# A fused attention and GEGLU kernel: merged output stores, three tiles of x turned by DMA, halved first units, a last tile in 384 and 128 columns

## The chip, the cores and the metric

The kernel runs on one core of one Trainium2 chip. The metric is the device time of one execution in microseconds (us), as a median of several. The span of a profile is a little shorter than the time of its run (325.7 us against 327.67 us for the kernel before), because it counts from the first to the last instruction.

## The reference

Eight batches of eight heads, 576 tokens and head size 64 go through linear attention with cosine weights. The result x, 4608 tokens x 512 columns, goes through a gated feed-forward layer:

```python
q_p, k_p = phi(q), phi(k)            # relu(x)*cos, relu(x)*sin, side by side: 64 -> 128 features
kv  = einsum('bhsf,bhsd->bhfd', k_p, v);  z = sum(k_p, axis=2)
x   = (q_p @ kv) / (q_p @ z + 1e-6)  # to 4608 x 512
out = (gelu(x @ w_gate) * (x @ w_val)) @ w_out     # 512 -> 1536 -> 512, float32 out
```

## The kernel before

The feed-forward work is cut into 9 blocks of 512 tokens (n), each of 12 gate/value units (jt). While block n is worked on, the attention of batch n+1 is done between its units: `kv_unit` and `nm_unit` make tiles of x, and x must be transposed into xT before the next block can read it. q is transposed too (`turn_q`). From batch 2 on the transposes of q, and from batch 3 on all of x, are done by DMA, issued by SyncE. All loads from batch 3 on are issued by SyncE as well, and so are the output stores. SyncE issues all of these in the order of the program, on one queue.

A token s of a batch is laid out as s = 9p + j, with p from 0 to 63 and j from 0 to 8. A tile of 128 output rows holds two values of j, 64 rows each. Rows of one j lie nine rows apart in memory. The kernel stores a tile in two transfers, one for each j:

```python
def flush():
    for i, o_sb in stores:                       # one output tile of 128 rows x 512 columns
        for half in range(2):
            b, j = divmod(2 * i + half, R)       # R = 9
            dst = out[b * S:(b + 1) * S, :].rearrange("(p j) c -> j p c", j=R)[j]   # 64 x 512
            nc.sync.dma_start(out=dst, in_=o_sb[64 * half:64 * half + 64])
    stores.clear()

def turn_q(b):                                   # q of a batch, transposed by DMA
    for i in range(2):
        nc.sync.dma_start_transpose(out=qt_tile(b)[:, i]..., in_=phi["q", b][64 * i:64 * i + 64]...)

def turn_x(b, t):                                # one tile of x, transposed by DMA
    x = xs.pop((b, t))
    for blk, c, o, m in pieces(b, t):
        nc.sync.dma_start_transpose(out=xT_block(blk)[:, :, c:c + m], in_=x[o:o + m, :])

# turn_x_pe(b, t, bank, copy): the same by four TensorE transposes and a copy
# ... in the loop over blocks, n == 1:
#     turn_x_pe(b, i, 5, act_copy)     for the three first tiles of batch 2
```

Of the kernel before, what the change touches and what calls it, by code (L numbers as in the profile page):

```python
# [16 lines left out]
def kernel(  # L17
# [13 lines left out]
    nc = tc.nc  # L31

    B, H, S, D = q.shape
    F = 2 * D
    C = H * D
# [4 lines left out]
    R = S // 64  # L40
    NB = B * S // 512
# [22 lines left out]
    def bank(i):  # L64
        return ps[:, i]

    def bank16(i):
        return ps[:, i].bitcast(BF16)
# [8 lines left out]
    def load(eng, name, b, m0, m1, j0=0, j1=R):  # L77
        if (name, b) not in staged:
            staged[name, b] = inp.tile([128, NP, R * D], FP32, name=name + "f")
        eng.dma_start(  # L80
            out=staged[name, b][:, m0:m1, j0 * D:j1 * D],
            in_=rows(srcs[name], b)[:, m0:m1, j0 * D:j1 * D],
        )
# [3 lines left out]
    wo_sb = weights.tile([128, JT, C], BF16)  # L87
# [53 lines left out]
    act_copy, dve_copy, pool_copy = nc.scalar.copy, nc.vector.tensor_copy, nc.gpsimd.tensor_copy  # L141
# [35 lines left out]
    def cast_v(b, m0, m1, copy, j0=0, j1=R):  # L177
        copy(  # L178
            vx_tiles[b % 2][:, m0:m1, j0:j1, 0:D],
            staged["v", b][:, m0:m1, j0 * D:j1 * D].rearrange("p m (j d) -> p m j d", d=D),  # L180
        )
# [149 lines left out]
    def xT_block(blk):  # L331
        if blk not in xT:
            xT[blk] = xtp.tile([128, CT, BLK], BF16, name="xT")
        return xT[blk]

    def pieces(b, t):

        o = max(128 * (t + 1) - S, 0)
        c0, n = b * S + t * 128, 128 - o
        while n > 0:  # L340
            m = min(n, BLK - c0 % BLK)
            yield c0 // BLK, c0 % BLK, o, m
            c0, o, n = c0 + m, o + m, n - m

    def turn_x(b, t):
        x = xs.pop((b, t))
        for blk, c, o, m in pieces(b, t):
            nc.sync.dma_start_transpose(
                out=xT_block(blk)[:, :, c:c + m], in_=x[o:o + m, :]
            )  # L350

    def turn_x_pe(b, t, to, copy):
        x = xs.pop((b, t))
        p = bank16(to)[:, 0:CT * 128].rearrange("p (c n) -> p c n", c=CT)
        for ct in range(CT):
            nc.tensor.transpose(  # L356
                out=p[:, ct, :], in_=x[:, ct * 128:(ct + 1) * 128], identity=ident
            )
        for blk, c, o, m in pieces(b, t):
            copy(xT_block(blk)[:, :, c:c + m], p[:, :, o:o + m])  # L360
# [5 lines left out]
    def gv_unit(n, jt, c0=0, w=BLK):  # L366
        xt = xT[n]
        js = slice(jt * 128, (jt + 1) * 128)
        b0 = 2 * (turn[0] % 2)
        turn[0] += 1  # L370
        if n not in hT:
            hT[n] = ffn.tile([128, JT, BLK], BF16, name="hT")
        for g, wt in ((0, wg_sb), (1, wv_sb)):
            for ct in range(CT):
                nc.tensor.matmul(  # L375
                    bank(b0 + g)[:, 0:w],
                    lhsT=wt[:, ct, js],
                    rhs=xt[:, ct, c0:c0 + w],
                    start=(ct == 0),
                    stop=(ct == CT - 1),  # L380
                )
        gel = ffn.tile([128, BLK], FP32, name="gel")
        nc.scalar.activation(gel[:, 0:w], bank(b0)[:, 0:w], AF.Gelu)  # L383
        nc.vector.tensor_mul(  # L384
            hT[n][:, jt, c0:c0 + w], gel[:, 0:w], bank(b0 + 1)[:, 0:w]
        )

    stores = []

    def flush():  # L390
        for i, o_sb in stores:
            for half in range(2):
                b, j = divmod(2 * i + half, R)
                dst = out[b * S:(b + 1) * S, :].rearrange("(p j) c -> j p c", j=R)[j]
                nc.sync.dma_start(out=dst, in_=o_sb[64 * half:64 * half + 64])
        stores.clear()

    def o_part(i, jts, to, copy):
# [164 lines left out]
    def loads(b, names=("q", "k", "v")):  # L563
        for name in names:
            for m in (0, 2):
                load(nc.sync, name, b, m, m + 2)
# [12 lines left out]
    turn[0] = 1  # L579
    for n in range(1, NB):  # L580
        b = n + 1
        t_kv, t_nm, t_q, t_k = {1: (5, 8, 12, 12), 2: (4, 7, 7, 9), 3: (1, 5, 6, 9)}.get(
            n, (1, 2, 4, 8)
        )
        for jt in range(JT):
            if n > 2 or jt > 1:
                gv_unit(n, jt)
            else:
                for i in range(2):
                    gv_unit(n, i, jt * HALF, HALF)  # L590
                    if n == 1:
                        j = JA + 2 * jt + i
                        prep("q", b, 1, (j,), eng=nc.scalar)
                        prep("q", b, 0, (j,))
                        if jt == i == 0:
                            turn_x_pe(1, 3, 5, act_copy)
            if jt % 3 == 1:
                flush()
            if b < B:
                if n == 1 and jt == 2:  # L600
                    prep("q", b, 0, (R - 1,))
                    prep("q", b, 1, (R - 1,), eng=nc.scalar)
                    turn_q(b)
                    nm_unit(1, NT - 1)
                if n == 1 and jt == 3:
                    turn_x(1, NT - 1)
                    loads(b + 1, ("k", "v"))

                late = -(-(BLK - 64 * b) // 128)
                nms = [(b, jt - t_nm)] if 0 <= jt - t_nm < (late if n == 1 else NT) else []  # L610
                if n == 2 and jt < 2:
                    nms.append((n, 3 + jt))
                i = jt - t_nm - 1
                if 0 <= i < late:
                    if n == 1:
                        turn_x_pe(b, i, 5, act_copy)
                    else:
                        turn_x(b, i)
                for bt in nms:
                    nm_unit(*bt)  # L620
                if jt == t_kv:
                    kv_unit(b)
                i = jt - (2, 1)[n - 1] if n <= 2 else -1
                if 0 <= i < 3:
                    prep_third("k", b, i)
                if n == 2 and jt in (2, 3):
                    cast_v(b, 2 * jt - 4, 2 * jt - 2, dve_copy)
                i = jt - (10 if n == 2 else 9)
                if n > 1 and 0 <= i < 2 and b + 1 < B:
                    cast_v(b + 1, 2 * i, 2 * i + 2, dve_copy)  # L630
                if (n, jt) in q3:
                    cosines, sines_ = q3[n, jt]
                    prep("q", 3, 1, sines_, eng=nc.scalar)
                    prep("q", 3, 0, cosines)
                if n > 1 and b + 1 < B:
                    if 0 <= jt - t_q < 3:
                        prep_third("q", b + 1, jt - t_q)
                    if 0 <= jt - t_k < 3:
                        prep_third("k", b + 1, jt - t_k)
                for c, t in nms:  # L640
                    if t == NT - 1:
                        if c + 1 < B:
                            turn_q(c + 1)
                        if c + 2 < B:
                            loads(c + 2)
                        for i in range(-(-(BLK - 64 * c) // 128), NT):
                            turn_x(c, i)
            if n > 1:
                o_part(
                    4 * (n - 1) + jt // 3,  # L650
                    range(4 * (jt % 3), 4 * (jt % 3) + 4),
                    4,
                    act_copy,
                )
# [3 lines left out]


    o_sb = outp.tile([128, C], FP32, name="o_sb")  # L660
    for half, to, copy in ((0, 4, dve_copy), (1, 5, dve_copy)):
        cols = slice(256 * half, 256 * half + 256)
        for jt in range(JT):
            nc.tensor.matmul(  # L664
                bank(to)[:, 0:256],
                lhsT=hT[NB - 1][:, jt, 384:512],
                rhs=wo_sb[:, jt, cols],
                start=(jt == 0),
                stop=(jt == JT - 1),
            )  # L670
        copy(o_sb[:, cols], bank(to)[:, 0:256])  # L671
        for i, eng in ((0, nc.sync), (1, nc.scalar)):
            b, j = divmod(8 * NB - 2 + i, R)
            dst = out[b * S:(b + 1) * S, cols].rearrange("(p j) c -> j p c", j=R)[j]
            eng.dma_start(out=dst, in_=o_sb[64 * i:64 * i + 64, cols])


# [28 lines left out]
```

## Time and profile before

| | before |
|---|---|
| time, median of 6 runs | 327.67 us (327.36 to 329.83) |
| TensorE busy | 318.1 us of 325.7 (98%) |
| share of TensorE in the chain that ended last | 94% |
| end of the last matmul, end of the span | 321.9 us, 325.7 us |

These are lines of the profile page of the kernel before: the busy time of the engines, the granted TensorE clock (the share of its full speed that the chip let TensorE run at) and the DMA engines' busy share in 40 equal slices (each digit is in tenths), two of the DMA queues (packets, MB, share of 16 engines' time), the chain that ended last by engine, and the store's issues (count, KB each, median us from issue to landing).

```profile
PE 318.1 (98%) x2434; PEld 163.9 (50%) x2434; DVE 167.6 (51%) x404; ACT 161.3 (50%) x342; POOL 28.4 (9%) x43
PEclk9999999999999999999999999999999999999999
DMA  7999999988199989959978992764521111111124
...
q1 hardware_dynamic: 57632, 40.84, 54.3%
...
q10 hardware_dynamic: 160, 0.13, 0.2%
...
PE 94%; DMA 3%; DVE 1%; SPq 1%; issue 0%; DVEq 0%
...
out_dram<-o_sb SPq DMA_DIRECT2D x70, 128.0 KB, 2.5
```

TensorE is the limit. It hardly ever waits, and its mean granted clock is 0.999. The DMA row is the second thing to see: up to the 26th slice the DMA engines are nearly full in many slices, then they are almost idle. So DMA is hidden in the first two thirds, without much room. q1 is SyncE's queue and q10 ScalarE's. q10 holds two stores here, of the last tile, and their 160 packets are worth a count: 128 rows of data, and 32 packets of 4 bytes, which I read as the marks of completion: the last of them starts at 324.27 us, after the last row at 324.23 us. That is 16 marks for each store. The 3104 packets of 4 bytes on q1 add up the same way: 16 for each of 72 stores and 36 loads, 32 for each of 43 transposes.

### The profile page before, as it was taken

How to read it: one execution, taken by the hardware profiler on the slowest of the kernel's cores; microseconds unless marked ns; L12 is line 12 of the kernel's file. 1: busy time of each engine (PE TensorE's matmuls, PEld its weight loads, DVE VectorE, ACT ScalarE, POOL GpSimd, SP SyncE). 2: the span in 40 equal slices, each digit the busy share in tenths (PEclk: the TensorE clock that was granted, in tenths of full speed). 3: DMA queues.
4: the chain of work that ended last, by engine and by line, in shares of the span. 5: the costliest groups of instructions: out<-in, count | busy, mean ns of one | idle time of the engine just before them, and what ended most of it. 6: DMA issues, size and time to landing. Idle time of an engine off the chain costs nothing.

```text
span 325.7 us, 6315 instructions
## 1 busy us (share of the span) xinstructions
PE 318.1 (98%) x2434; PEld 163.9 (50%) x2434; DVE 167.6 (51%) x404; ACT 161.3 (50%) x342; POOL 28.4 (9%) x43
## 2 busy tenths in 40 slices
PE   8799999999999999999999999999999999999995
PEld 3585556556554454545544545445544444444443
DVE  5864667848845942794485448544532222222211
ACT  8764758948645833574466336642222233222220
POOL 2855462000000000000000000000000000000000
PEclk9999999999999999999999999999999999999999
DMA  7999999988199989959978992764521111111124
GB/s 275 250 191 274 307 346 340 213 128 290 30 135 369 213 102 290 306 103 179 360 160 118 309 296 47 100 108 100 90 65 40 35 32 32 34 33 32 34 64 98
DMA packets 67471, 53.17 MB, mean 163 GB/s; under 512 B 43761, under 2 KB 52721, under 8 KB 67441
## 3 DMA queue, kind: packets, MB, share of 16 engines
q1 hardware_dynamic: 57632, 40.84, 54.3%
q0 software_dynamic: 9648, 11.80, 15.8%
q8 instruction: 19, 0.31, 0.4%
q10 hardware_dynamic: 160, 0.13, 0.2%
q14 instruction: 12, 0.09, 0.1%
HBM read 37.75 MB, written 9.44 MB: 145 GB/s over the span
## 4 chain that ended last, share of the span: by engine, by line
PE 94%; DMA 3%; DVE 1%; SPq 1%; issue 0%; DVEq 0%
PE ps L375 57%; PE ps L401 28%; PE ps L281 3%; DMA qf<-in_q_dram 3%; PE ps L240 3%; PE ps L356 1%; PE ps L664 1%; SPq L80 1%; PE ps L203 1%; DVE qp L161 0%; DVE x_sb L321 0%; DVE o_sb L671 0%; DVE rec L317 0%; PE ps L139 0%; DVE den L316 0%
## 5 line engine op out<-in xcount | busy, mean ns | idle before, releaser
L384 DVE TENSOR_TENSOR hT<-gel,ps 128x512 bf16<-128x512 f32 (+2 forms) x118 | 75.5, 642 | 133.3 <-PE ps L375 129.4
L383 ACT ACTIVATE gel<-ps 128x512 f32<-128x512 f32 (+2 forms) x118 | 66.2, 562 | 107.6 <-PE ps L375 106.1
L375 PE MATMUL ps<-xT,wg_sb 128*128 128x512 bf16 (+2 forms) x472 | 112.6, 361 | 0.4 <-issue 0.4
L375 PE MATMUL ps<-xT,wv_sb 128*128 128x512 bf16 (+2 forms) x472 | 112.6, 361 | 0.0
L401 PE MATMUL ps<-wo_sb,hT 128*128 128x512 bf16 x420 | 105.9, 379 | 0.0
L375 PEld LDWEIGHTS <-wv_sb 128*128 128x128 bf16 x472 | 45.7, 98 | 47.9
L375 PEld LDWEIGHTS <-wg_sb 128*128 128x128 bf16 x472 | 44.9, 98 | 46.5 <-DMA out_dram<-o_sb 0.9
L401 PEld LDWEIGHTS <-hT 128*128 128x128 bf16 x420 | 38.4, 98 | 40.2
L410 ACT COPY o_sb<-ps 128x512 f32<-128x512 f32 x34 | 19.9, 586 | 31.3 <-PE ps L401 31.3
L159 ACT ACTIVATE qp<-qf,sin_t 128x256 bf16<-128x256 f32 x71 | 31.9, 503 | 1.0 <-DMA qf<-in_q_dram 0.8
L159 ACT ACTIVATE kp<-kf,sin_t 128x256 bf16<-128x256 f32 (+1 forms) x75 | 30.4, 477 | 0.4 <-DMA kf<-in_k_dram 0.4
L294 DVE TENSOR_TENSOR x_sb<-ps,rec 128x512 bf16<-128x512 f32 x38 | 26.3, 691 | 1.3
L161 DVE TENSOR_SCALAR qp<-qf,cos_t 128x256 bf16<-128x256 f32 x71 | 21.8, 355 | 4.2 <-ACT kv_sb L249 3.3
L161 DVE TENSOR_SCALAR kp<-kf,cos_t 128x256 bf16<-128x256 f32 x63 | 18.1, 347 | 0.0
L281 PEld LDWEIGHTS <-qT 128*128 128x128 bf16 x304 | 14.5, 98 | 7.1
L281 PE MATMUL ps<-kv_sb,qT 128*128 128x65 bf16 x304 | 16.0, 194 | 0.0
L249 ACT CAST kv_sb<-ps 128x260 bf16<-128x260 f32 x14 | 4.6, 382 | 13.1 <-PE ps L240 13.1
L139 PE MATMUL ps<-dummy 128*128 128x512 bf16 x30 | 8.9, 434 | 1.5 <-POOL dummy L113 1.5
L240 PEld LDWEIGHTS <-kp 64*128 64x128 bf16 x504 | 8.6, 94 | 3.1 <-issue 3.0
L178 DVE CAST vx<-vf 128x1152 bf16<-128x1152 f32 x12 | 9.2, 768 | 0.8 <-DMA vf<-in_v_dram 0.8
L240 PE MATMUL ps<-vx,kp 64*128 64x65 bf16 x504 | 9.5, 191 | 0.0
L293 DVE RECIPROCAL rec<-den 128x8 f32<-128x8 f32 x38 | 7.7, 203 | 1.3
(52 smaller groups left out, 95.4 us busy)
## 6 DMA issues: line engine op xcount, KB each, us to landing
out_dram<-o_sb SPq DMA_DIRECT2D x70, 128.0 KB, 2.5
kf<-in_k_dram SPq DMA_DIRECT2D x12, 576.0 KB, 6.8
vf<-in_v_dram SPq DMA_DIRECT2D x12, 576.0 KB, 8.9
qf<-in_q_dram SPq DMA_DIRECT2D x10, 576.0 KB, 5.0
qf<-in_q_dram POOLq DMA_DIRECT2D x4, 576.0 KB, 12.1
kf<-in_k_dram POOLq DMA_DIRECT2D x4, 576.0 KB, 12.8
vf<-in_v_dram POOLq DMA_DIRECT2D x4, 576.0 KB, 10.8
wg_sb<-in_moe_w_gate_dram POOLq DMA_DIRECT2D x6, 256.0 KB, 8.7
```

What stands on the lines that cost most here:

```text
L139: nc.tensor.matmul(bank(to), lhsT=dummy[:, 0:128], rhs=dummy, start=True, stop=True)
L159: nc.scalar.activation(o, i, AF.Relu, scale=tab[:, j:j + 1])
L161: (eng or nc.vector).tensor_scalar(o, i, 0.0, tab[:, j:j + 1], op0=ALU.max, op1=ALU.mult)
L178: copy(vx_tiles[b % 2][:, m0:m1, j0:j1, 0:D], staged["v", b][:, m0:m1, j0 * D:j1 * D].rearrange("p m (j d) -> p m j d", d=D),)
L240: nc.tensor.matmul(bank(6 + i)[:, m * (D + 1):(m + 1) * (D + 1)], lhsT=kp[rr, m, j, :], rhs=vx[rr, m, j, :], start=(j == 0), stop=(j == R ...
L281: nc.tensor.matmul(bank(b0 + h // 4)[:, (h % 4) * (D + 1):(h % 4 + 1) * (D + 1)], lhsT=q_cols(b, t, h), rhs=kv_sb[b][:, h // 2, h % 2, :], ...
L294: nc.vector.tensor_tensor(x, nm[:, :, :, 0:D], rec[:, :, :, None].to_broadcast([128, 2, 4, D]), op=ALU.mult,)
L375: nc.tensor.matmul(bank(b0 + g)[:, 0:w], lhsT=wt[:, ct, js], rhs=xt[:, ct, c0:c0 + w], start=(ct == 0), stop=(ct == CT - 1),)
L383: nc.scalar.activation(gel[:, 0:w], bank(b0)[:, 0:w], AF.Gelu)
L384: nc.vector.tensor_mul(hT[n][:, jt, c0:c0 + w], gel[:, 0:w], bank(b0 + 1)[:, 0:w])
L401: nc.tensor.matmul(bank(to), lhsT=hT[n][:, jt, tt * 128:(tt + 1) * 128], rhs=wo_sb[:, jt, :], start=(jt == 0), stop=(jt == JT - 1),)
L410: copy(o_sb, bank(to))
```

## The change

Four things were meant to take small pieces of work from the path. Batch 2's three tiles of x go by DMA instead of TensorE, with v(3)'s load moved behind them in the queue. Block 3's first two units are done in halves of 256 columns, so that the first can begin before all of xT is there (some casts and one `kv_unit` move with it). A tile goes out in one store of 256 KB in place of two of 128 KB. The last tile is done in 384 and 128 columns, so that the final copy and store are smaller. The core of the diff:

```diff
+    def store(eng, i, o_sb, c0=0, c1=C):
+        b, j = divmod(2 * i, R)
+        if j + 1 < R:
+            dst = out[b * S:(b + 1) * S, c0:c1].rearrange("(p j) c -> j p c", j=R)[j:j + 2]
+            eng.dma_start(out=dst, in_=o_sb[:, c0:c1])          # 2 x 64 x 512  <-  128 x 512
+        else:                                                   # tiles 4, 13, 22, 31: two batches
+            for n in range(2):
+                ...                                             # 64 x 512, as before
     def flush():
         for i, o_sb in stores:
-            for half in range(2): ...
+            store(nc.sync, i, o_sb)
...
-        t_kv, ... = {..., 3: (1, 5, 6, 9)}
+        t_kv, ... = {..., 3: (2, 5, 6, 9)}
-            if n > 2 or jt > 1:
+            if n > 3 or jt > 1:
                 gv_unit(n, jt)
...
-                    loads(b + 1, ("k", "v"))
+                    loads(b + 1, ("k",))
...
-                    if n == 1:
-                        turn_x_pe(b, i, 5, act_copy)
-                    else:
-                        turn_x(b, i)
+                    turn_x(b, i)
+                    if n == 1 and i == late - 1:
+                        loads(b + 1, ("v",))
... (casts of v moved)
-    for half, to, copy in ((0, 4, dve_copy), (1, 5, dve_copy)):      # last tile: 256 + 256
+    for c0, c1, to in ((0, C - 128, 4), (C - 128, C, 5)):            # 384 + 128
...
+        store(nc.scalar if c0 == 0 else nc.sync, 4 * NB - 1, o_sb, c0, c1)
```

More of the change, by code (lines that the diff above doesn't have):

```diff
@@ L388 @@
     stores = []
+    def store(eng, i, o_sb, c0=0, c1=C):
[5 more added lines that the diff above has]
+            for n in range(2):
+                b, j = divmod(2 * i + n, R)
+                dst = out[b * S:(b + 1) * S, c0:c1].rearrange("(p j) c -> j p c", j=R)[j]
+                eng.dma_start(out=dst, in_=o_sb[64 * n:64 * n + 64, c0:c1])
     def flush():
         for i, o_sb in stores:
-            for half in range(2):
-                b, j = divmod(2 * i + half, R)
-                dst = out[b * S:(b + 1) * S, :].rearrange("(p j) c -> j p c", j=R)[j]
-                nc.sync.dma_start(out=dst, in_=o_sb[64 * half:64 * half + 64])
+            store(nc.sync, i, o_sb)
         stores.clear()
@@ L581 @@
         b = n + 1
-        t_kv, t_nm, t_q, t_k = {1: (5, 8, 12, 12), 2: (4, 7, 7, 9), 3: (1, 5, 6, 9)}.get(
+        t_kv, t_nm, t_q, t_k = {1: (5, 8, 12, 12), 2: (4, 7, 7, 9), 3: (2, 5, 6, 9)}.get(
             n, (1, 2, 4, 8)
@@ L625 @@
                     prep_third("k", b, i)
-                if n == 2 and jt in (2, 3):
-                    cast_v(b, 2 * jt - 4, 2 * jt - 2, dve_copy)
-                i = jt - (10 if n == 2 else 9)
-                if n > 1 and 0 <= i < 2 and b + 1 < B:
+                i = jt - (2 if n == 2 else 0)
+                if n in (2, 3) and 0 <= i < 2:
+                    cast_v(b, 2 * i, 2 * i + 2, dve_copy)
+                i = jt - 9
+                if n > 2 and 0 <= i < 2 and b + 1 < B:
                     cast_v(b + 1, 2 * i, 2 * i + 2, dve_copy)
@@ L660 @@
     o_sb = outp.tile([128, C], FP32, name="o_sb")
-    for half, to, copy in ((0, 4, dve_copy), (1, 5, dve_copy)):
-        cols = slice(256 * half, 256 * half + 256)
+    for c0, c1, to in ((0, C - 128, 4), (C - 128, C, 5)):
         for jt in range(JT):
             nc.tensor.matmul(
-                bank(to)[:, 0:256],
+                bank(to)[:, 0:c1 - c0],
                 lhsT=hT[NB - 1][:, jt, 384:512],
-                rhs=wo_sb[:, jt, cols],
+                rhs=wo_sb[:, jt, c0:c1],
                 start=(jt == 0),
@@ L670 @@
             )
-        copy(o_sb[:, cols], bank(to)[:, 0:256])
-        for i, eng in ((0, nc.sync), (1, nc.scalar)):
-            b, j = divmod(8 * NB - 2 + i, R)
-            dst = out[b * S:(b + 1) * S, cols].rearrange("(p j) c -> j p c", j=R)[j]
-            eng.dma_start(out=dst, in_=o_sb[64 * i:64 * i + 64, cols])
+        nc.vector.tensor_copy(o_sb[:, c0:c1], bank(to)[:, 0:c1 - c0])
+        store(nc.scalar if c0 == 0 else nc.sync, 4 * NB - 1, o_sb, c0, c1)
 _INS = ['q', 'k', 'v', 'moe_w_gate', 'moe_w_val', 'moe_w_out']
```

## The prediction

> **What bounds it now.** TensorE. The busy table gives it 318.1 of 325.7 us, the granted clock is 0.999, and the chain of waits is 94% TensorE (57% gate/value matmuls, 28% output matmuls). From the second output block on the chain runs without a gap: 1.73 us for a gate/value unit, 0.86 us for four output matmuls, about 33.7 us per block with attention work, 31.1 us without. DMA is hidden, but with little room: by the stretches view its busy share is 0.82 to 0.98 between 52 and 181 us.
>
> **Small items, all cheap.** Three tiles of batch 2 no longer go through TensorE: 12 transposes (16 took 0.89 us in the chain, so about 0.7 us) and three ScalarE copies of about 0.59 us, off the path. Their DMA transposes land in 3.1 us median, with some 4 us to spare. v(3) is loaded about 20 us later; its cast in the second unit of block 2 might wait 1 or 2 us. Halving two units of block 3 costs nothing (16 half matmuls took 1.75 us against 1.73 for 8 whole). The last tile in 384 + 128 columns shortens its final copy (0.42 us now) by about 0.1 us. One store instead of two saves SyncE issues of 0.59 us that nothing waits for. Alone: -1 us, within 2%.
>
> **What I think decides it: the shape of the new store.** In the built program its destination has the sizes 2 x 64 x 512, its source 128 x 512. [...] No transfer of the trace before has such a shape, so the trace neither confirms nor denies it. Of 36 tiles, 32 get this store (tiles 4, 13, 22 and 31 keep two stores).
>
> Estimate: a 2 KB store packet takes 81 to 84 ns in the trace [...], so 64 on one engine take 5.2 us. Per block with attention the two engines also carry their sixteenth of the loads (9 to 11 us by packet durations), of the q transposes (about 9 us) and of the x transposes (about 4 us): with four stores 43 us against 33.7. [...] x, q and k for later blocks wait behind stores; slack of about 10 us is used up early, then TensorE waits for transposed x or q in blocks 1 to 5. Summed and with slack deducted: about 24 us. In the last 15 us tiles 32 to 34 finish every 2.6 us but each store needs 5.2 us on the same two engines: the end slips about 11 us past the last matmul's normal end.
>
> **Predicted: 362 us, 335 to 390.** Faster by over 2%: 0.03, within 2%: 0.10, slower: 0.87.
>
> **What would show it.** Stores landing in 6 us or more instead of 2.5; the DMA share at the end near 2/16 = 0.12 and some 10 us of it after the last matmul; TensorE gaps of several us in blocks 1 to 5, with transposes of x or q, or their loads, as releasers; the chain with tens of us of DMA. Packet counts of 2 KB stay the same. TensorE busy time falls by under 1 us.
>
> **What would make it wrong.** If stores still use 16 engines, the time is 326 to 329 us. If blocks 1 to 5 have more slack than I count, only the tail of about 11 us remains (340 us). If a lone engine's store packets take 100 ns or more beside loads, it is 385 us or above.

The sum takes the two engines as given, and that was an assumption: 64 of a store's 128 packets on each, 5.2 us. It came to -1 us for the small items, 24 us in the middle and 11 us at the end, 34 us on 327.67, or 362 us. (Of the 4480 packets of 2 KB before, 1648 took at most 84 ns. They are not those beside which little else ran: from 238 to 312 us, with the stores nearly alone, the median is 149 ns.)

## More of the kernel before

The timeline of SyncE's DMA issues of the kernel before, in block 1 (start us, duration us, then what was issued and how often):

```profile
51.71 4.28 SPq L395 DMA_DIRECT2D out_dram<-o_sb  x6
56.16 1.00 SPq L80 DMA_DIRECT2D qf<-in_q_dram  x2
57.27 1.15 SPq L395 DMA_DIRECT2D out_dram<-o_sb  x2
61.86 8.18 SPq L192 DMA_TRANSPOSE qT<-qp  x2
70.13 1.82 SPq L348 DMA_TRANSPOSE xT<-x_sb  x1
```

Six stores (three tiles) are issued first. The two loads behind them are issued in 1.00 us, and both transposes of q in 8.18 us.

## The result, and the profile after

The changed kernel is correct and slower: 371.88 us (369.31 to 373.22, 6 runs) against 327.67 us. The ratio is 1.1326, with a 95% interval of 1.1277 to 1.1374. Ratios here are the mean time of one kernel's runs over that of the other's of the same rounds, so they are not quite the ratio of the medians quoted. Executions over 1.5% slower than the fastest of the same kernel are left out of the means.

The lines of the changed kernel's profile page that answer to those above:

```profile
PE 322.6 (87%) x2401; PEld 166.1 (45%) x2438; DVE 168.4 (46%) x406; ACT 159.8 (43%) x341; POOL 28.4 (8%) x43
PEclk9999999965999989998999999999999999999965
DMA  8999992967599999879997999895194111111211
...
q1 hardware_dynamic: 58304, 41.17, 60.3%
...
q10 hardware_dynamic: 130, 0.20, 0.1%
...
PE 70%; DMA 13%; SPq 7%; DVE 2%; issue 1%; ACT 1%; DVEq 0%; ACTq 0%
...
out_dram<-o_sb SPq DMA_DIRECT2D x31, 256.0 KB
```

Look at q10 first. It holds one store now, the last tile's 384 columns: 128 rows of data, and 130 - 128 = 2 completion marks in place of 16, at 364.66 and 364.68 us, after the last row at 364.54 us. I take this for the number of DMA engines that the store ran on; experiment 3 tests it. The page gives no time to landing any more for the stores. The chain has 70% TensorE, and DMA and SyncE's queue have 20% of it.

The stretches view tells the same without counting marks. A stretch in which one tile's store is the only traffic, first in the kernel before (two transfers of 64 x 512), then in the changed one (one transfer; the second line is tile 31, which keeps its two transfers; the third is the tail). Columns: stretch, its length, busy us of the five engines with instruction counts, granted clock, DMA share, GB/s.

```profile
297.71:299.06 1.35, 1.35 (x8) 0.63 (x7) 0.69 (x1) 0.00 (x0) 0.00 (x0) 1.00 0.84 194
```

```profile
335.10:341.35 6.25, 6.20 (x30) 2.83 (x30) 2.06 (x3) 1.44 (x3) 0.00 (x0) 1.00 0.15 46
343.00:344.30 1.30, 1.30 (x8) 0.59 (x6) 0.00 (x0) 0.59 (x1) 0.00 (x0) 1.00 0.80 183
345.00:367.70 22.70, 6.46 (x42) 3.49 (x40) 1.54 (x3) 0.59 (x1) 0.00 (x0) 0.70 0.13 46
```

The same 256 KB take 1.35 us at a DMA share of 0.84, and 6.25 us at 0.15. Two engines of 16 are 0.125. Counted from the packets in the trace, at most 16 of the store's 2 KB packets were in flight at once before, and at most 3 after (neighbours overlap a little). Each packet has become shorter, 84 ns at the median against 134 ns before, but by the marks 64 of them now stand in line on one engine where 8 did.

Are they the same two engines each time? The tail says so. There three merged stores of SyncE wait one behind another, and yet at most 4 of their packets are in flight at once. The last tile's store on ScalarE's queue runs beside them from 355.7 to 364.6 us. Just before, SyncE's 2 KB packets start at about 25 per us. Beside it they start at 14 per us, and so do ScalarE's 1.5 KB packets: two of one queue, two of the other, in turns (two on q1 at 358.23 us, two on q10 at 358.31, two on q1 at 358.37), and at most 3 of both together are in flight. My reading is that both queues use the same two engines, and that each engine takes one packet of each in turn.

Now what this does to the others in the queue. SyncE's issues in block 1 of the changed kernel:

```profile
51.89 3.00 SPq L395 DMA_DIRECT2D out_dram<-o_sb  x3
55.08 8.50 SPq L80 DMA_DIRECT2D qf<-in_q_dram  x2
63.68 1.22 SPq L395 DMA_DIRECT2D out_dram<-o_sb  x1
65.07 17.52 SPq L192 DMA_TRANSPOSE qT<-qp  x2
82.69 2.00 SPq L348 DMA_TRANSPOSE xT<-x_sb  x1
```

They are the same transfers as before, in the same order, with one store for a tile in place of two. The two loads behind the first three merged stores take SyncE 8.50 us to issue instead of 1.00, and the transposes of q behind the fourth take 17.52 us instead of 8.18. The TensorE timeline shows the bill (in brackets: the idle time before, and what ended it):

```profile
71.98 1.03 PE L375 MATMUL ps<-xT,wv_sb 128*128 128x512 bf16 x4
80.89 0.24 PE L281 MATMUL ps<-kv_sb,qT 128*128 128x65 bf16 x1 [7.88 <-DMA qT<-qp]
85.39 0.57 PE L281 MATMUL ps<-kv_sb,qT 128*128 128x65 bf16 x7 [4.26 <-DMA qT<-qp]
85.76 1.90 PE L375 MATMUL ps<-xT,wg_sb 128*128 128x512 bf16 x4
87.45 1.92 PE L375 MATMUL ps<-xT,wv_sb 128*128 128x512 bf16 x4
```

TensorE waits 7.88 and 4.26 us for q's transposes. Then four matmuls take 1.90 us where they took 1.03: the clock has been taken back. From 77.6 to 91.2 us the granted clock is 0.50, and PEclk is 6 and 5 in those two slices. Later a wait of 2.56 us, too, was followed by such a fall. Its line of the TensorE timeline, and the stretches view of the 3.4 us that followed, in which the granted clock is 0.50:

```profile
131.13 0.61 PE L375 MATMUL ps<-xT,wg_sb 128*128 128x256 bf16 x4 [2.56 <-DMA xT<-x_sb]
```

```profile
132.20:135.60 3.40, 3.27 (x12) 1.35 (x10) 1.51 (x3) 0.38 (x1) 0.00 (x0) 0.50 1.71 68
```

Waits of 1.58 and 1.25 us in the same trace (ending at 137.0 and 230.7 us) were not followed by a fall.

How the loss of 43.9 us of span is spread. The lengths of the blocks are read from the multiplications that end the gate/value units, twelve to a block:

| part | before, us | after, us | difference |
|---|---|---|---|
| up to the end of block 0 | 40.4 | 40.6 | +0.2 |
| block 1 | 39.7 | 54.5 | +14.8 |
| block 2 | 34.0 | 33.1 | -0.9 |
| block 3 | 33.9 | 40.1 | +6.2 |
| block 4 | 33.8 | 39.2 | +5.4 |
| block 5 | 33.7 | 37.1 | +3.4 |
| blocks 6 to 8 | 95.9 | 96.8 | +0.9 |
| end of the last matmul | 321.9 | 351.5 | +29.6 |
| from there to the end of the span | 3.8 | 18.2 | +14.4 |

TensorE's idle time between its first and its last matmul rose from 2.2 to 27.3 us. The other 4.5 us of the 29.6 are in its busy time (322.6 against 318.1): matmuls at the lower clock. This split is rough, because the trace after lacks 37 matmul records (2401 for 2438 weight loads), which makes busy time look idle. The trace of the merged store alone (experiment 2) lacks none (2434 for 2434), and there the busy time is 324.9 us, 6.8 us more than before.

### The profile page after: what moved, and what is told of

It reads as the page before. It is cut to its first block, busy times and chain, and to the rows that moved or that the text cites. A ratio compares the mean times of both kernels' runs of the same rounds, so it can differ in the third digit from the quotient of the medians.

```text
span 369.6 us, 6259 instructions
## 1 busy us (share of the span) xinstructions
PE 322.6 (87%) x2401; PEld 166.1 (45%) x2438; DVE 168.4 (46%) x406; ACT 159.8 (43%) x341; POOL 28.4 (8%) x43
## 4 chain that ended last, share of the span: by engine, by line
PE 70%; DMA 13%; SPq 7%; DVE 2%; issue 1%; ACT 1%; DVEq 0%; ACTq 0%
PE ps L375 44%; PE ps L410 21%; DMA xT<-x_sb 6%; DMA qT<-qp 4%; SPq L192 3%; DMA qf<-in_q_dram 3%; PE ps L281 2%; SPq L80 2%; PE ps L240 2%; SPq L348 2%; DMA out_dram<-o_sb 1%; PE ps L672 1%; DVE qp L161 1%; PE ps L203 1%; PE ps L356 1%
## 5 line engine op out<-in xcount | busy, mean ns | idle before, releaser
L375 PE MATMUL ps<-xT,wg_sb 128*128 128x512 bf16 (+2 forms) x472 | 114.3, 362 | 9.6 <-DMA xT<-x_sb 8.8
L375 PE MATMUL ps<-xT,wv_sb 128*128 128x512 bf16 (+2 forms) x473 | 114.3, 362 | 0.3
L410 PE MATMUL ps<-wo_sb,hT 128*128 128x512 bf16 x400 | 104.3, 384 | 2.8 <-ACT o_sb L419 1.3
L375 PEld LDWEIGHTS <-wg_sb 128*128 128x128 bf16 x480 | 46.0, 99 | 57.1 <-issue 7.5
L375 PEld LDWEIGHTS <-wv_sb 128*128 128x128 bf16 x480 | 46.9, 99 | 48.5 <-issue 1.9
L419 ACT COPY o_sb<-ps 128x512 f32<-128x512 f32 x34 | 19.9, 586 | 34.7 <-PE ps L410 27.3
L281 PE MATMUL ps<-kv_sb,qT 128*128 128x65 bf16 x304 | 16.9, 196 | 13.1 <-DMA qT<-qp 13.1
L292 DVE TENSOR_SCALAR den<-ps 128x8 f32<-128x8 f32 x38 | 6.1, 159 | 12.6 <-PE ps L281 12.4
## 6 DMA issues: line engine op xcount, KB each, us to landing
qf<-in_q_dram POOLq DMA_DIRECT2D x4, 576.0 KB, 12.2
```

What stands on the lines that cost most here:

```text
L281: nc.tensor.matmul(bank(b0 + h // 4)[:, (h % 4) * (D + 1):(h % 4 + 1) * (D + 1)], lhsT=q_cols(b, t, h), rhs=kv_sb[b][:, h // 2, h % 2, :], ...
L375: nc.tensor.matmul(bank(b0 + g)[:, 0:w], lhsT=wt[:, ct, js], rhs=xt[:, ct, c0:c0 + w], start=(ct == 0), stop=(ct == CT - 1),)
L410: nc.tensor.matmul(bank(to), lhsT=hT[n][:, jt, tt * 128:(tt + 1) * 128], rhs=wo_sb[:, jt, :], start=(jt == 0), stop=(jt == JT - 1),)
L419: copy(o_sb, bank(to))
```

## The experiments

**Theory A**: the merged store runs on two DMA engines because its destination's outermost size is 2. All stores pile up on the same two, and loads and transposes, which are taken to run on all 16 (in the trace before a load leaves 16 completion marks and a transpose 32), wait in the queue behind them. **Rival B**: turning x by DMA, loading v(3) late and shifting the casts starve TensorE. **Rival C**: 256 KB transfers are worse than 128 KB ones, whatever their shape. All times below are medians; "last matmul" and "tail" (from there to the end of the span) are from each run's profile.

### 1. The changed kernel with two stores per tile

```diff
-        if j + 1 < R: one store of 2 x 64 x (c1 - c0)
-        else: two of 64 x (c1 - c0)
+        for n in range(2): one store of 64 x (c1 - c0) each, in every tile
```

> The changed kernel with only its store undone: every tile goes out in two stores of 64 x 512 (the last tile in two of 384 and two of 128 columns), all else as changed. Theory A (the merged store runs on 2 DMA engines): the whole loss goes, 325 to 328 us, ratio to before 0.992 to 1.000, nothing above 2 us after the tail as before. Rival B (x of batch 2 by DMA, v(3) loaded late and the shifted casts starve TensorE): it stays at 350 us or more. Rival C (256 KB transfers are worse than 128 KB ones, whatever their shape): also 325 to 328 us, so this run doesn't tell A from C.

Measured: 329.67 us against 329.28 for the kernel before, ratio 1.0008 (0.9968 to 1.0049). The whole loss is gone, so B falls. (The time lies 1.7 us above the range expected, 325 to 328 us, and the ratio just above its own; the kernel before, too, took 329.28 us in this round and not 327.67.) SyncE's issues in block 1 are back to what they were:

```profile
57.74 1.01 SPq L80 DMA_DIRECT2D qf<-in_q_dram  x2
63.48 8.09 SPq L192 DMA_TRANSPOSE qT<-qp  x2
```

What the other parts of the change bring together can't be told from nothing: the estimate of 1 us is smaller than the interval.

### 2. The kernel before with only the merged store

```diff
+            b, j = divmod(2 * i, R)
+            if j + 1 < R:
+                dst = out[...].rearrange("(p j) c -> j p c", j=R)[j:j + 2]
+                nc.sync.dma_start(out=dst, in_=o_sb)
+                continue
             for half in range(2): ...
```

> The kernel before with only the merged store (2 x 64 x 512) in all tiles but 4, 13, 22, 31 and the last. Theory A: 360 to 375 us, with stores' time on two engines and TensorE waiting for x and q transposes. Rival B: 326 to 330 us. Rival C: as A.

Measured: 368.33 us, ratio 1.1170 (1.1121 to 1.1220). The merged store alone brings nearly the whole loss. It is a little less than 1.1326 partly because the last tile keeps its stores as they were before (16 completion marks each in that trace): the tail is 13.1 us here instead of 18.2.

### 3. One store of 256 KB, with other outermost sizes

The four runs keep one store per tile but write it to 128 consecutive rows, as a x (128/a) x 512. The rows of the output are in wrong places on purpose; bytes, packets and the number of transfers are those of a merged store.

```diff
-        b, j = divmod(2 * i, R)
-        ... (the stores as changed)
+        dst = out[128 * i:128 * i + 128, c0:c1].rearrange("(p a) c -> a p c", a=A)   # A = 2, 4, 8, 16
+        eng.dma_start(out=dst, in_=o_sb[:, c0:c1])
```

> The changed kernel, its one store of 256 KB per tile kept, but the destination's outermost size is 16 (16 x 8 x 512, onto 128 consecutive rows, so the rows of the output are in wrong places on purpose). Theory A: 325 to 328 us, as with two stores; the transfer is as large as in the changed kernel but runs on 16 engines. Rival C: 360 us or more.

> As the run with outermost size 16, but 4 (4 x 32 x 512; wrong rows on purpose). Theory A: 4 engines, each with 32 packets of 84 ns or 2.7 us per tile; four tiles are 11 us of a block of 33.7 us beside some 22 us of other work, so DMA just fits: 326 to 336 us, the tail up to 2 us longer than before. Rival C: 360 us or more, the same as with any outermost size.

> As the runs with outermost size 16 and 4, but 2 (2 x 64 x 512 onto 128 consecutive rows, step of two rows; wrong rows on purpose). It tells the outermost size from the rows' places in memory. Theory A: two engines again, in all 36 tiles: 370 to 380 us. If the far steps of nine rows in the changed kernel were to blame: 326 to 330 us.

> As the runs with outermost size 2 (383.8 us), 4 (343.8 us) and 16 (328.3 us), but 8 (8 x 16 x 512; wrong rows on purpose). Theory A: 8 engines with 16 packets of 84 ns, 1.35 us per tile, so 5 us of a block of 33.7: the engines have room again, 327 to 331 us, after the last matmul at most 6 us.

| outermost size | time, us | ratio to before (95%) | last matmul, us | tail, us |
|---|---|---|---|---|
| 2 | 383.84 | 1.1670 (1.1614 to 1.1725) | 359.9 | 20.1 |
| 4 | 343.80 | 1.0433 (1.0386 to 1.0479) | 330.1 | 10.3 |
| 8 | 331.73 | 1.0073 (1.0028 to 1.0117) | 323.9 | 5.8 |
| 16 | 328.34 | 0.9962 (0.9914 to 1.0011) | 324.4 | 4.0 |

The line of ScalarE's queue in the four profile pages (packets, MB, share), in the order 2, 4, 8, 16; each holds one store of the last tile's 384 columns, 128 rows:

```profile
q10 hardware_dynamic: 130, 0.20, 0.1%
```

```profile
q10 hardware_dynamic: 132, 0.20, 0.2%
```

```profile
q10 hardware_dynamic: 136, 0.20, 0.2%
```

```profile
q10 hardware_dynamic: 144, 0.20, 0.2%
```

Less the 128 rows of data, that is 2, 4, 8 and 16 completion marks: the outermost size, each time. A transfer of 256 KB with outermost size 16 costs nothing that can be told from noise, so C falls. And with outermost size 2 the loss is there whether the rows lie two apart (383.84 us) or nine (371.88 us), so it isn't the places in memory. Only the outermost size of the destination was varied; that of the source is 128 in all four.

All four times lie outside the ranges expected, with 16 by 0.3 us alone (328.34 for 325 to 328). With 4 I expected 326 to 336 us and got 343.8. One reason can be read from the stretches view of that run, where one store of 256 KB is alone:

```profile
290.50:294.85 4.35, 4.35 (x22) 1.99 (x21) 1.38 (x2) 0.69 (x2) 0.00 (x0) 1.00 0.25 64
```

A store took 4.35 us from first to last packet, not the 32 x 84 ns = 2.7 us that I had put in. I put the rest down to a slow start, as in the changed kernel's trace, where 16 packets of the store alone at 335.1 us started in its first us and about 24 per us from 337.6 us on. For the tail I had also left out that five tiles, 31 to 35, have to pass: four times 32 x 84 ns, then 32 x 65 ns and 32 x 27 ns for the last tile's two parts, are 13.7 us of packets on each engine, and they begin only at about 321 us. With 2 I expected at most 380 us and got 383.84; here tiles 4, 13, 22 and 31 run on two engines too. With 8 it was 331.73, 0.7 us above the range.

### 4. The last block's stores alone

```diff
-        if j + 1 < R:
+        if i < 32 and j + 1 < R:     # first run: two stores in the last block alone
+        if i >= 32 and j + 1 < R:    # second run: merged in the last block alone
```

> The changed kernel with two stores per tile for the last block's tiles alone (32 to 35), the merged store in all earlier ones. Theory A, with the loss split as the two traces split it (last matmul 29.6 us later, work after it 14.4 us longer): the part after the last matmul returns to about 4 us, so 356 to 360 us. If the stores' two engines mattered only in the middle or only at the end, it would be 372 or 328 us.

> The reverse: the merged store for tiles 32 to 35 alone, two stores in all earlier ones. Theory A: the last matmul as early as with two stores, some 18 us after it instead of 4, so 340 to 344 us.

Measured: 357.89 us (ratio 1.0893, 1.0843 to 1.0943) and 341.45 us (1.0386, 1.0332 to 1.0439). Both lie in their ranges. Without merged stores at the end, the last matmul ends at 351.3 us and the tail is 3.9 us. With them only at the end, it is 321.5 us, and the tail is 17.5 us. The two parts of the loss are separate, and nearly add up: they are 28.6 and 12.2 us above the 329.28 us of before, 40.8 us together, against 44.2 us in the changed kernel (371.88 less 327.67, in another round).

### 5. The merged stores on another queue

```diff
     def flush():
         for i, o_sb in stores:
-            store(nc.sync, i, o_sb)
+            store(nc.gpsimd, i, o_sb)
```

> The changed kernel with its merged stores (all but the last tile's) issued by the GpSimd queue instead of SyncE's, so they don't stand in the queue of the loads and transposes. If the loss comes from all stores on the same two engines' rings in order ahead of the transposes and loads (theory A as I state it), and this queue spreads two-engine transfers over different pairs, it is 328 to 340 us. If this queue uses the same two engines each time: 350 us or more. If a store over two engines were bad only by its own latency, nothing would change: about 370 us.

Measured: 368.11 us, the median of three runs (a fourth, 374.39 us, was slow), ratio 1.1242 (1.1154 to 1.1330). All stores but the last tile's went to this queue, those in two parts too. The hope of 328 to 340 us missed: another queue does not help, so the order in SyncE's queue is not needed for the loss. By time alone the run doesn't tell a queue that uses the same two engines each time from a store that is bad only by its own latency (about 370 us), but the transposes are seen to slow down. While a store is under way on this queue (its packets are 4 KB, 159 ns each), their packets, 256 bytes each, come at 64 to 104 per us (x's at 126 to 128 us, q's at 131 to 135 us), where q's transposes without a store beside them run at about 530 (97 to 100 us). In the first us of a store they can still run at 470 to 531 (123 and 129 us). The stretches view of this run, first with a store under way, then with the transposes alone (the last two columns are DMA share and GB/s):

```profile
124.00:128.00 4.00, 0.85 (x4) 0.10 (x1) 1.01 (x4) 1.05 (x3) 0.80 (x1) 0.55 0.79 65
97.00:99.90 2.90, 2.90 (x16) 1.28 (x14) 2.46 (x6) 2.03 (x5) 1.14 (x2) 1.00 1.03 136
```

The engines are busy in both, but move 65 GB/s in the first and 136 in the second. My reading is that the engines with a store take turns between the two queues packet by packet, and so hold up a transfer that runs on all 16. The tail of the changed kernel shows such turns for the queues of SyncE and ScalarE. Here the rates fit, as an estimate: 12 store packets per us on two engines are 6 for each, and 95 transpose packets on 16 engines are 5.9 for each. It is not shown directly, for which engine a packet used, the trace doesn't say. In the tail 16 to 20 of the 4 KB packets started per us, where two engines alone manage 13, so the stores there were not all on the same two. The part of theory A that says "all on the same two" thus needn't hold for this queue, and the loss is there all the same.

### 6. The small parts: x of batch 2 back on TensorE

```diff
+                    if n == 1:
+                        turn_x_pe(b, i, 5, act_copy)
+                    else:
-                    turn_x(b, i)
+                        turn_x(b, i)
```
(on top of the two stores of experiment 1)

> Two stores per tile and, in addition, x of batch 2 turned by TensorE and ScalarE as in the kernel before; v(3) late, halves of block 3 and the last tile's 384 and 128 columns as changed. If the 1.29 us wait at the start of block 2 in the run with two stores comes from the DMA transposes, it goes, and 12 transposes (0.7 us) come back: 0.5 us faster than that run, ratio to before 0.993 to 1.003, too little to tell apart by time, but the wait must be gone from the trace. If it comes from the halves or from v(3), it stays.

Measured: 328.98 us, ratio 0.9989 (0.9955 to 1.0024), the same as before. The TensorE timelines at the start of block 2, first with DMA transposes (experiment 1), then with TensorE's:

```profile
81.75 0.60 PE L375 MATMUL ps<-xT,wg_sb 128*128 128x256 bf16 x4 [1.29 <-DMA xT<-x_sb]
```

```profile
80.12 0.39 PE L356 MATMUL ps<-ident,x_sb 128*128 128x128 bf16 x4
80.35 0.60 PE L375 MATMUL ps<-xT,wg_sb 128*128 128x256 bf16 x4
```

The wait of 1.29 us is gone with the transposes back on TensorE. But the wait is not the same in every run: in the run with merged stores at the end only, which has the DMA transposes, it was 0.56 us and put down to another engine. So moving these tiles to DMA swaps 0.7 us of TensorE work for a wait of 0.6 to 1.4 us in the traces; no time here is fine enough to tell which is better. No version was found that beats the kernel before by more than the noise.

## Why the prediction was right

The measured 371.88 us lies in the range of 335 to 390, 10 us above the forecast of 362. Point by point:

- **Two engines per merged store**: right. It is shown by the completion marks (2 in place of 16), by the DMA share of 0.15 while one store is alone, by at most 3 of its packets in flight, and by the runs with outermost sizes 2, 4, 8 and 16.
- **5.2 us per store**: too small. From first to last packet it is 6.25 us; the packets take the 84 ns put in (64 of them are 5.4 us), but the store starts slowly (16 packets in its first us, about 24 per us from 2.5 us on).
- **The middle, about 24 us**: 29.6 us. The two terms missing were the slack and the clock. The "slack of about 10 us" was not there where it was needed: the first four merged stores and two loads stood directly ahead of q's transposes of batch 2, and block 1 lost 14.8 us at once. And with the waits of 7.88, 2.56 and 3.64 us came stretches at a granted clock of 0.50, which ended at 91.2, 135.6 and 176.6 us; TensorE's busy time was 4.5 us longer in this trace, 6.8 us in that of experiment 2. The prediction said that busy time would fall by under 1 us; this was wrong. The sum is in part luck: 43 against 33.7 us would be some 9 us a block once the slack is gone, but blocks 2 to 5 lost -0.9, 6.2, 5.4 and 3.4 us, so a first block that lost too much made up for later ones that lost less than that.
- **x, q and k wait behind stores**: transfers did wait behind them (8.50 us for 1.00), but standing in the same queue is not needed for the loss: with the stores in another queue it stayed (experiment 5).
- **The tail, about 11 us**: 14.4 us. Tiles 32 to 34 at 64 x 84 ns are 16.1 us on each engine, and the last tile's two stores, 64 x 65 ns and 64 x 27 ns, are 5.9 us more, which the estimate had left nearly out. They are 22.0 us together; the packets ran from 345 to 367.6 us.
- **The small items, -1 us**: not told apart from nothing (1.0008, 0.9968 to 1.0049). Of its terms, "some 4 us to spare" for x's transposes was wrong: TensorE waited 1.29 us in experiment 1. The late v(3) cost nothing: in that run VectorE waited 0.4 us for v, against 0.8 before.
- **What would show it**: 2 KB packets are 4480 in both traces, as said; the gaps are in the blocks named but for block 2, with q's and x's transposes as releasers; the last matmul is followed by more than the 10 us expected.

What the prediction rested on was one thing that the trace before could not show: that a store of this shape runs on two engines. It was an assumption until the runs; that the engines are as many as the outermost size is shown by the completion marks of experiment 3, for the sizes 2, 4, 8 and 16.

## What to carry to other kernels

Before merging DMA transfers, write down the destination's sizes as the instruction will carry them: here an outermost size of 2 put the whole transfer on two DMA engines (2 completion marks in place of 16, a DMA share of 0.15 in place of 0.84), and "one larger transfer" made the kernel 12% slower by itself. The harm was not only the transfer's own length: the loads and transposes near it slowed down as well (8.50 us for 1.00, 17.52 for 8.18), so look at what runs behind and beside it in time. In this kernel TensorE was busy for 98% of the span and waited for none of the transfers that were merged, so the merge had nothing to win: the changed kernel with stores on all 16 engines measured 0.9962 (0.9914 to 1.0011).
